# One more mirrored pair of score blocks turned by the DMA, and the second diagonal pair computed whole

## The chip, the cores and the metric

The kernel runs on one core of a Trainium2 chip. The metric is the time of one execution on the device in microseconds (us), the median of three runs.

## The reference

Two layers follow one another. The first is an attention without softmax over 8 batches of 2496 tokens. The second sends each of the 19968 tokens to one of eight experts.

```python
scores = (1.0 / S) * np.matmul(z, z.transpose(0, 2, 1))     # z: 8 x 2496 x 64
attn = np.maximum(scores, 0.0) ** 2
x = (u * np.matmul(attn, v)).reshape(B * S, D)              # u, v: 8 x 2496 x 256
...
expert_idx = np.argmax(x @ w_gate, axis=1)                  # 8 experts
h = np.maximum(xe @ w1[e], 0.0)                             # 256 -> 1024
out[mask] = gate_w[mask, None] * (h @ w2[e])                # 1024 -> 256
```

Two facts of it matter here. The score matrix of a batch is symmetric, since both factors are z: the block of keys A against queries B is the transpose of the block of keys B against queries A. And all inputs are 32-bit floats.

## The kernel before, in words

**Tiles.** A batch has five chunks of queries (`c` = 0 to 4), four of 512 and a last one of 448. Keys come in ten pairs of 128-key blocks (`kp` = 0 to 9), so chunk `cc` of the keys is made of the pairs `2*cc` and `2*cc+1`. One step is one (batch, chunk, pair): `scores` (lines 255 to 336) makes a tile of 2 x 128 keys by `n` queries, `weighted` (lines 338 to 349) multiplies it into the accumulator with v. There are 8 x 5 x 10 = 400 steps. To keep 32-bit accuracy each operand is held as a rounded part and a remainder (`hi` and `lo`), so a step of `weighted` takes 12 matmuls (10 in the step of the last pair).

**A step that computes its scores** has four matmuls into PSUM (lines 309 and 310), two ScalarE activations (Relu on line 318, Square on line 319) into a 32-bit tile `a`, and on VectorE a rounding copy to `hi` (line 320) and a subtraction to `lo` (line 322, or lines 326 and 327 for the last pair).

**A step that takes its scores from the mirror** happens where the keys' chunk `cc` lies before the queries' chunk `c`: the block was computed earlier in the same batch, was kept in one of six slots of SBUF (`s0` to `s5`) and has only to be turned. There are two ways, chosen by `by_dma` (line 251):

- by TensorE: eight 128 x 128 transposes against an identity into PSUM (line 281), then one ScalarE copy to `hi` (line 282) and one VectorE subtraction (line 283). The pairs of chunks (0,3), (0,4), (1,4), (2,4) and (3,4) go this way.
- by the DMA: when the block is computed, ScalarE and VectorE write its upper and lower 16 bits into a tile `th` (lines 333 and 334), and SyncE issues one transposing DMA of that tile into the slot (line 335). When the block is used, ScalarE puts the upper halves back (line 266) and VectorE the lower ones (line 267), then come the copy to `hi` (line 268) and the subtraction (line 269). The pairs (0,1), (0,2), (1,2), (1,3) and (2,3) go this way.

**The diagonal.** Where `cc == c`, the two pairs of a chunk mirror each other in part. With `late` (chunks 1 to 3 of every batch, and chunk 0 of every batch but the first: 31 chunks) the first pair is kept in a tile of its own, `sd`; the second pair computes only its last 256 columns, and the first 256 come from `sd` by four transposes on TensorE (line 315), with a copy and a subtraction of their own (lines 316 and 317).

**Buffers and order.** `ring_f` (name `tf`) has three buffers, `ring_hi` and `ring_lo` four each, the PSUM tiles of the scores (`ps_s`) two, `th` three. `scores` runs three steps ahead of `weighted`. `order_of` (line 228) sets the order of the pairs: the chunk's second diagonal pair goes last, and after the first batch the last chunk goes 0, 2, 3, 4, 5, 6, 7, 8, 9, 1. A scheduler then settles where each instruction stands in its engine's queue, and each queue is worked off in order. SyncE's queue also holds the turning of the output rows (line 393), the loads of z, u and v (lines 120, 150, 137) and the stores of the rows (line 474). The attention is followed by the experts (lines 765 to 819), which use other lines of the kernel.

## Time and profile before

| quantity | value |
|---|---|
| runs | 2329.19, 2334.91, 2337.47 us; median 2334.91 |
| the profiled execution | 2345.85 us, its span 2344.1 us |
| mean granted TensorE clock | 0.992 |
| end of the last chunk's attention in the span | about 1392 us |
| TensorE, VectorE, ScalarE, GpSimd busy | 98%, 70%, 58%, 27% of the span |
| transposing DMAs into slots (line 335) | 80 |
| transposes on TensorE, line 281 and line 315 | 640 and 124 |

The profile is of one execution. PE is TensorE, DVE VectorE, ACT ScalarE, POOL GpSimd, SP SyncE. A matmul's duration in the trace contains a part that overlaps the next matmul, so what a matmul costs is read from one start to the next. `<-` in brackets names what ended the idle time before an instruction. The name of a tile is given without its buffer's number in the trace.

### The profile page before, as it was taken

What the parts mean: (1) busy time and instruction counts of PE and PEld (TensorE: products, weight loads), DVE (VectorE), ACT (ScalarE), POOL (GpSimd) and SP (SyncE); (2) the same over time, 40 slices, a digit from 0 to 9 for tenths busy, and PEclk for the clock granted to TensorE, in tenths of its full rate; (3) what the DMA queues carried; (4) which work ended last, traced back from release to release, by engine and by line L of the source; (5) the groups of instructions that cost most, each with busy time, mean ns of one, the idle gap of its engine ahead of it and who ended that gap; (6) DMA issues with size and microseconds to landing.
All of it is one profiled execution on the core that took longest, in us unless ns stands there. A gap on an engine that the chain in (4) does not pass through costs nothing. (4 is left out here: it accounts for less than half of the span.)

```text
span 2344.1 us, 33779 instructions
## 1 busy us (share of the span) xinstructions
PE 2299.6 (98%) x12448; PEld 1944.4 (83%) x12448; DVE 1652.4 (70%) x2955; ACT 1368.4 (58%) x1864; POOL 625.1 (27%) x637
## 2 busy tenths in 40 slices
PE   9999999999999999999999999899999999999998
PEld 6887888888888888888888887688888888888887
DVE  8877868868868868868878767555565656657554
ACT  7647647647647647657657645354555555546443
POOL 4010110110110211201101234543454435345322
PEclk9999999999999999999999999999999999999999
DMA  6435636536536438447346485655566557456620
GB/s 160 91 64 114 116 59 131 104 67 139 98 72 135 96 68 139 88 72 149 74 73 125 107 156 102 171 145 135 159 163 165 165 128 205 129 145 190 156 77 28
DMA packets 421085, 278.92 MB, mean 119 GB/s; under 512 B 355820, under 2 KB 377850, under 8 KB 411696
## 3 DMA queue, kind: packets, MB, share of 16 engines
q1 hardware_dynamic: 389520, 157.59, 35.5%
q0 software_dynamic: 31392, 119.10, 17.2%
q8 instruction: 99, 1.62, 0.3%
q14 instruction: 74, 0.61, 0.1%
HBM read 149.79 MB, written 43.43 MB: 82 GB/s over the span
## 5 line engine op out<-in xcount | busy, mean ns | idle before, releaser
L349 PE MATMUL acc<-thi,t 128*128 128x512 f32 (+1 forms) x1600 | 617.4, 387 | 0.0
L346 PE MATMUL acc<-thi,t 128*128 128x512 f32 (+1 forms) x1600 | 607.3, 393 | 1.3 <-DVE thi L320 1.3
L348 PE MATMUL acc<-tlo,t 128*128 128x512 f32 (+1 forms) x1520 | 588.8, 387 | 5.2 <-DVE tlo L322 5.2
L784 DVE SCALAR_TENSOR_TENSOR t<-ph,t 128x512 fp32r<-128x512 f32 (+1 forms) x328 | 220.3, 674 | 254.3 <-ACT t L783 218.4
L779 PE MATMUL ph<-thi,t 128*128 128x512 f32 (+2 forms) x1248 | 381.5, 362 | 14.6 <-DVE t L784 12.1
L800 PE MATMUL y<-t,t 128*128 128x512 f32 x1062 | 384.0, 398 | 1.8 <-ACT t L783 1.4
L783 ACT ACTIVATE t<-ph 128x512 fp32r<-128x512 f32 (+1 forms) x328 | 191.7, 588 | 302.6 <-PE ph L779 207.7
L349 PEld LDWEIGHTS acc<-thi,t 128*128 128x128 f32 x1600 | 301.4, 188 | 55.1
L346 PEld LDWEIGHTS acc<-thi,t 128*128 128x128 f32 x1600 | 300.8, 189 | 52.9 <-DVE thi L320 1.7
L348 PEld LDWEIGHTS acc<-tlo,t 128*128 128x128 f32 x1520 | 286.8, 189 | 58.4 <-DVE tlo L322 9.0
L479 POOL DMA_INDIRECT lst<-toks,posi x160 | 180.0, 1125 | 464.5 <-DVE posi L471 423.7
L802 PE MATMUL y<-t,t 128*128 128x256 f32 x1062 | 296.1, 282 | 0.5 <-DVE t L784 0.5
L779 PEld LDWEIGHTS ph<-thi,t 128*128 128x128 f32 x1248 | 226.7, 190 | 58.0 <-DVE t L784 14.0
L800 PEld LDWEIGHTS y<-t,t 128*128 128x128 f32 x1062 | 200.6, 189 | 45.9 <-ACT t L783 1.9
L779 PE MATMUL ph<-tlo,t 128*128 128x512 f32 (+2 forms) x624 | 225.4, 361 | 3.9 <-issue 3.9
L814 POOL DMA_INDIRECT out_dram<-tf,lfidx x136 | 143.3, 1054 | 266.4 <-DVE tf L812 236.5
L802 PEld LDWEIGHTS y<-t,t 128*128 128x128 f32 x1062 | 201.4, 190 | 11.8 <-DVE t L784 1.8
L310 PE MATMUL ps_s<-t,t 128*128 128x512 f32 (+1 forms) x480 | 178.4, 375 | 0.0
L318 ACT ACTIVATE tf<-ps_s 128x1024 f32<-128x1024 f32 (+2 forms) x129 | 117.3, 909 | 76.4 <-PE ps_s L310 39.1
L383 POOL MEMSET rows<- 128x64 int32 x40 | 10.5, 266 | 527.8 <-DMA xrows<-rows 326.6
L714 POOL DMA_INDIRECT rows<-xrows,lfidx x136 | 137.5, 1011 | 44.6 <-issue 37.5
L320 DVE CAST thi<-tf 128x1024 fp32r<-128x1024 f32 (+2 forms) x129 | 81.8, 636 | 87.5 <-ACT tf L319 74.5
(252 smaller groups left out, 4093.0 us busy)
## 6 DMA issues: line engine op xcount, KB each, us to landing
vr<-in_v_dram SPq DMA_DIRECT2D x80, 256.0 KB
xrows<-rows SPq DMA_DIRECT2D x32, 544.0 KB
u<-in_ut_dram SPq DMA_DIRECT2D x32, 512.0 KB
zr<-in_zt_dram SPq DMA_DIRECT2D x38, 256.0 KB
u<-in_ut_dram SPq DMA_DIRECT2D x8, 448.0 KB
xrows<-rows SPq DMA_DIRECT2D x8, 408.0 KB
rows<-th SPq DMA_TRANSPOSE x160
lst<-toks,posi POOLq DMA_INDIRECT x160
```

What stands on the lines that cost most here:

```text
L310: nc.tensor.matmul(ps[:, i, m:n], lhsT=hl_k, rhs=lh_q[:, m:n], start=False, stop=True)
L346: nc.tensor.matmul(acc[d][:, :n], lhsT=vh, rhs=hi[:, i, :n], start=first and i == 0, stop=False)
L348: nc.tensor.matmul(acc[d][:, :n], lhsT=vh, rhs=lo[:, i, :n], start=False, stop=False)
L349: nc.tensor.matmul(acc[d][:, :n], lhsT=vl, rhs=hi[:, i, :n], start=False, stop=last and i == 1)
L479: i = nc.gpsimd.indirect_dma_start(out=lst1, out_offset=bass.IndirectOffsetOnAxis(ap=posi[:m, j:j + 1], axis=0), in_=toks[:m, col + j:col ...
L714: nc.gpsimd.indirect_dma_start(out=xg[:, s, :], out_offset=None, in_=src, in_offset=bass.IndirectOffsetOnAxis(ap=lists[which]["idx"][:, s, ...
L779: nc.tensor.matmul(o, lhsT=w1[:, part, dd, fs], rhs=xx[:, dd, :n], start=p == 0, stop=p == 5)
L783: nc.scalar.activation(hh[:, :m], ph[:, :m], AF.Relu)
L784: nc.vector.scalar_tensor_tensor(hl[:, :m], ph[:, :m], 0.0, hh[:, :m].bitcast(F32), op0=ALU.max, op1=ALU.subtract)
L800: nc.tensor.matmul(y, lhsT=hh[:, cs], rhs=w2[:, f % 2].rearrange("p i d -> p (i d)"), start=f == 0, stop=False)
L802: nc.tensor.matmul(y[:, 0:D], lhsT=hl[:, cs], rhs=w2[:, f % 2, 0, :], start=False, stop=f == NF - 1)
L814: d = nc.gpsimd.indirect_dma_start(out=out, out_offset=bass.IndirectOffsetOnAxis(ap=lists[which]["idx"][:, s, t:t + 1], axis=0), in_=yo[:, ...
```

## The change

`by_dma` now also holds for (3,4): the block that chunk 3 computes for the keys of chunk 4 (pairs 8 and 9) is split into halves and turned by two DMAs while chunk 3 runs, and chunk 4 puts it together again in its steps of the pairs 6 and 7. In the last chunk both copies of line 267's kind are ScalarE's. And the second diagonal pair computes all its columns; `late`, `sd`'s use in the attention, the four transposes and the two instructions of lines 316 and 317 are gone, and the first diagonal pair writes to `ring_f`.

```diff
     def by_dma(c, cc):
-        return c < cc < NC_ - 1 and (c, cc) != (0, 3)
+        return c < cc < NC_ - 1 and (c, cc) != (0, 3) or (c, cc) == (NC_ - 2, NC_ - 1)
...
-            nc.vector.tensor_copy(dst[:, 0], st[:, 1, js])
+            (nc.scalar.copy if c == NC_ - 1 else nc.vector.tensor_copy)(dst[:, 0], st[:, 1, js])
...
-        late = 0 < c < NC_ - 1 or b and c == 0
...
-        elif late and kp % 2 == 0:
-            sd = ring_sd().bitcast(F32).rearrange("p s r -> p (s r)")[:, 0:2 * QC]
-            a = stored[b, c, c] = sd.rearrange("p (i n) -> p i n", i=2)
         else:
             a = ring_f()
...
-        m = HQ if cc == c and late and kp % 2 else 0
         for i in range(2):
...
-            nc.tensor.matmul(ps[:, i, m:n], lhsT=hl_k, rhs=hl_q[:, m:n], start=True, stop=False)
-            nc.tensor.matmul(ps[:, i, m:n], lhsT=hl_k, rhs=lh_q[:, m:n], start=False, stop=True)
-        if m:
-            st = stored.pop((b, c, c))
...
-                    nc.tensor.transpose(ps[:, i, r * P:(r + 1) * P], st[:, r, HQ + i * P:HQ + (i + 1) * P], ident)
-            nc.scalar.copy(hi[:, :, 0:m], ps[:, :, 0:m])
-            nc.vector.tensor_tensor(lo[:, :, 0:m], ps[:, :, 0:m], hi[:, :, 0:m].bitcast(F32), op=ALU.subtract)
+            nc.tensor.matmul(ps[:, i, :n], lhsT=hl_k, rhs=hl_q[:, :n], start=True, stop=False)
+            nc.tensor.matmul(ps[:, i, :n], lhsT=hl_k, rhs=lh_q[:, :n], start=False, stop=True)
```

The activations, the rounding copy and the subtraction behind these lines lose their `m` likewise and work on all `n` columns.

The change moves instructions in three queues. The new kernel has twelve lines less, so line 318 of before is line 306 there, 319 is 307, 333 is 321, 335 is 323, 346 is 334, 393 is 381, 431 is 419 and 474 is 462; lines 266 to 268 and 282 keep their numbers.

On TensorE, the second diagonal pair of chunk 1 of the first batch before; `t` are the parts of z and of v, 128x256 is the half that is computed:

```order
L349 MATMUL acc_520<-thi,t_362 128x512
L309 MATMUL ps_s<-t_143 128x256
L310 MATMUL ps_s<-t_144,t_143 128x256
L309 MATMUL ps_s<-t_143 128x256
L310 MATMUL ps_s<-t_144,t_143 128x256
L315 MATMUL ps_s<-ident,sd 128x128 x4
L346 MATMUL acc_519<-thi,t_476 128x512
```

And now:

```order
L337 MATMUL acc_520<-thi,t_362 128x512
L304 MATMUL ps_s<-t_143 128x512
L305 MATMUL ps_s<-t_144,t_143 128x512
L304 MATMUL ps_s<-t_143 128x512
L305 MATMUL ps_s<-t_144,t_143 128x512
L334 MATMUL acc_519<-thi,t_476 128x512
```

The four matmuls have twice the columns, and the four transposes behind them are gone.

On ScalarE, the end of chunk 3 and the start of chunk 4 in the second batch before; the first four rows are the pairs 8 and 9 of chunk 3, whose block goes straight into slot `s1`, the next three the second diagonal pair, and `2x448` are the casts of mirrored steps of chunk 4:

```order
L318 ACTIVATE s1_3049<-ps_s_3048 128x1024
L319 ACTIVATE s1_3049<-s1_3049 128x1024
L318 ACTIVATE s1_3049<-ps_s_3078 128x1024
L319 ACTIVATE s1_3049<-s1_3049 128x1024
L316 CAST thi_3100<-ps_s_3102 128x2x256
L318 ACTIVATE tf_3103<-ps_s_3102 128x2x256
L319 ACTIVATE tf_3103<-tf_3103 128x2x256
L282 CAST thi_3139<-ps_s_3141 128x2x448
L431 ACTIVATE ex_2923<-dl_3132 128x32
L282 CAST thi_3165<-ps_s_3167 128x2x448
```

And now, from pair 9 on:

```order
L306 ACTIVATE tf_3046<-ps_s_3045 128x1024
L307 ACTIVATE tf_3046<-tf_3046 128x1024
L321 COPY th_3056<-tf_3046 128x2x512
L306 ACTIVATE tf_3075<-ps_s_3074 128x1024
L307 ACTIVATE tf_3075<-tf_3075 128x1024
L282 CAST thi_3105<-ps_s_3107 128x2x448
L266 COPY tf_3276<-s1_3011 128x1024
L267 COPY tf_3276<-s1_3011 128x1024
L266 COPY tf_3329<-s1_3011 128x1024
L267 COPY tf_3329<-s1_3011 128x1024
L419 ACTIVATE ex_2885<-dl_3098 128x32
L282 CAST thi_3131<-ps_s_3133 128x2x448
```

The four copies out of slot `s1`, which belong to the sixth and seventh step of chunk 4, stand right behind the cast of its first step and ahead of that of its second. So it is in the batches 0 to 6; in the last batch they stand ahead of the first cast too.

On SyncE, the stretch of chunk 3 in the second batch before, from the last transposing DMA of the pair (2,3):

```order
L335 DMA_TRANSPOSE s3_2640<-th_2738 128x16x128
L120 DMA zr_3338<-in_zt_dram 128x512
L474 DMA xrows_72<-rows_2586 128x4x272
L150 DMA u_2965<-in_ut_dram 128x2x512
L393 DMA_TRANSPOSE rows_2921<-th_3039 128x4x128 x4
L120 DMA zr_3667<-in_zt_dram 128x512
L474 DMA xrows_72<-rows_2921 128x4x272
L150 DMA u_3306<-in_ut_dram 128x2x448
```

And now:

```order
L323 DMA_TRANSPOSE s3_2608<-th_2706 128x16x128
L120 DMA zr_3298<-in_zt_dram 128x512
L462 DMA xrows_72<-rows_2554 128x4x272
L150 DMA u_2927<-in_ut_dram 128x2x512
L381 DMA_TRANSPOSE rows_2883<-th_3001 128x4x128 x4
L323 DMA_TRANSPOSE s1_3011<-th_3021 128x16x128
L120 DMA zr_3621<-in_zt_dram 128x512
L323 DMA_TRANSPOSE s1_3011<-th_3056 128x16x128
L462 DMA xrows_72<-rows_2883 128x4x272
L150 DMA u_3272<-in_ut_dram 128x2x448
```

One new transposing DMA stands between the turned rows and the load of z, the other behind that load.

More of the change, by code (lines that the diff above doesn't have):

```diff
@@ L308, in scores @@
             hl_k = ztiles[b, k // 4][0][:, (k % 4) * P:(k % 4 + 1) * P]
-            nc.tensor.matmul(ps[:, i, m:n], lhsT=hl_k, rhs=hl_q[:, m:n], start=True, stop=False)
-            nc.tensor.matmul(ps[:, i, m:n], lhsT=hl_k, rhs=lh_q[:, m:n], start=False, stop=True)
-        if m:
-            st = stored.pop((b, c, c))
-            for i in range(2):
-                for r in range(2):
-                    nc.tensor.transpose(ps[:, i, r * P:(r + 1) * P], st[:, r, HQ + i * P:HQ + (i + 1) * P], ident)
-            nc.scalar.copy(hi[:, :, 0:m], ps[:, :, 0:m])
-            nc.vector.tensor_tensor(lo[:, :, 0:m], ps[:, :, 0:m], hi[:, :, 0:m].bitcast(F32), op=ALU.subtract)
-        nc.scalar.activation(a[:, :, m:n], ps[:, :, m:n], AF.Relu)
-        nc.scalar.activation(a[:, :, m:n], a[:, :, m:n], AF.Square)
-        nc.vector.tensor_copy(hi[:, :, m:n], a[:, :, m:n])
+            nc.tensor.matmul(ps[:, i, :n], lhsT=hl_k, rhs=hl_q[:, :n], start=True, stop=False)
+            nc.tensor.matmul(ps[:, i, :n], lhsT=hl_k, rhs=lh_q[:, :n], start=False, stop=True)
+        nc.scalar.activation(a[:, :, :n], ps[:, :, :n], AF.Relu)
+        nc.scalar.activation(a[:, :, :n], a[:, :, :n], AF.Square)
+        nc.vector.tensor_copy(hi[:, :, :n], a[:, :, :n])
         if kp < NKP - 1:
-            nc.vector.tensor_tensor(lo[:, :, m:n], a[:, :, m:n], hi[:, :, m:n].bitcast(F32), op=ALU.subtract)
+            nc.vector.tensor_tensor(lo[:, :, :n], a[:, :, :n], hi[:, :, :n].bitcast(F32), op=ALU.subtract)
         else:
```

## The prediction

> **What bounds the kernel now.** I read the busy times first, then the stretches, then TensorE's own waits, and last the timeline at the steps that the change touches. The page's first part names the engine with the least room:
>
> ```profile
> PE 2299.6 (98%) x12448; PEld 1944.4 (83%) x12448; DVE 1652.4 (70%) x2955; ACT 1368.4 (58%) x1864; POOL 625.1 (27%) x637
> ```
>
> An average hides stages, so here are stretches (length, then the busy time of PE, PEld, DVE, ACT, POOL, then the granted clock and the DMA): the attention, the experts' stage, ten microseconds at the start of the second batch, and about its chunks 3 and 4.
>
> ```profile
> 0.00:1392.00 1392.00, 1379.15 (x7529) 1154.36 (x7530) 1094.12 (x1890) 873.33 (x993) 228.07 (x251) 1.00 0.53 103
> 1392.00:2344.00 952.00, 920.45 (x4921) 790.04 (x4919) 558.32 (x1065) 495.03 (x872) 397.04 (x386) 0.99 0.53 143
> 200.00:210.00 10.00, 8.21 (x50) 6.53 (x51) 7.78 (x15) 1.75 (x2) 1.69 (x3) 0.83 0.85 184
> 280.00:315.00 35.00, 35.00 (x192) 29.03 (x191) 27.05 (x45) 20.83 (x22) 4.17 (x5) 1.00 0.48 71
> 315.00:350.00 35.00, 35.00 (x221) 31.18 (x221) 21.00 (x38) 11.85 (x17) 4.03 (x5) 1.00 0.48 55
> ```
>
> In the attention TensorE is idle for 12.9 of 1392 us, in the experts' stage for 31.6 of 952. In chunks 3 and 4 it has no idle time at all, while ScalarE has 14 and 23 us of 35 to spare and VectorE 8 and 14. What TensorE does wait for inside the attention is short (total, times, longest):
>
> ```profile
> PE acc L348 <- DVE tlo L322: 5.2, 4, 2.3
> PE ps_s L309 <- ACT sd L318: 1.5, 2, 0.8
> ```
>
> So a microsecond of work taken from TensorE in the attention is a microsecond of time, unless the work that replaces it makes TensorE wait.
>
> **The turned pair: what TensorE saves.** The transposes before the change, and one such step of chunk 4 in the timeline (start, duration):
>
> ```profile
> L281 PE MATMUL ps_s<-ident,s 128*128 128x128 f32 x640 | 86.9, 275 | 0.2 <-DVE tlo L283 0.2
> L315 PE MATMUL ps_s<-ident,sd 128*128 128x128 f32 x124 | 18.6, 272 | 0.0
> ```
>
> ```profile
> 331.09 1.03 PE L281 MATMUL ps_s<-ident,s 128*128 128x128 f32 x8
> 331.88 0.45 PE L346 MATMUL acc<-thi,t 128*128 128x448 f32 x1
> 332.37 0.37 PE L349 MATMUL acc<-thi,t 128*128 128x448 f32 x1
> 333.59 0.37 PE L349 MATMUL acc<-thi,t 128*128 128x448 f32 x1
> ```
>
> From 332.37 to 333.59 lie six matmuls, 0.203 us each; that is the pace, not the 0.37 of the duration column. From 331.09 to 332.37, 1.28 us, lie eight transposes and two matmuls, so the eight cost 1.28 - 0.41 = 0.87 us, the slower start of the matmul behind them included. Five pairs of chunks share the 640 transposes; (3,4) has 128 of them, 16 times eight. The saving is 16 x 0.87 = 14.0 us, all on the path.
>
> **The diagonal: what TensorE pays and saves.** The second diagonal pair in chunk 1 of the first batch:
>
> ```profile
> 71.69 0.39 PE L348 MATMUL acc<-tlo,t 128*128 128x512 f32 x1
> 73.96 0.39 PE L349 MATMUL acc<-thi,t 128*128 128x512 f32 x1
> 74.18 0.28 PE L309 MATMUL ps_s<-t 128*128 128x256 f32 x1
> 74.66 0.60 PE L315 MATMUL ps_s<-ident,sd 128*128 128x128 f32 x4
> 75.01 0.48 PE L346 MATMUL acc<-thi,t 128*128 128x512 f32 x1
> 75.33 0.39 PE L348 MATMUL acc<-tlo,t 128*128 128x512 f32 x1
> ```
>
> Ten matmuls of 512 columns take 73.96 - 71.69 = 2.27 us, 0.227 each. The half pair takes 74.66 - 74.18 = 0.48 us for four matmuls and 75.33 - 74.66 - 0.227 = 0.44 us for four transposes, 0.92 together. Whole, it takes 4 x 0.227 = 0.91 us. The 124 transposes are four each in 31 places: 31 x 0.015 = 0.5 us saved. For TensorE this edit is a draw.
>
> **What ScalarE and VectorE get.** The groups of like instructions (busy in total, mean ns of one):
>
> ```profile
> L266 ACT COPY tf<-s 128x1024 uint16<-128x1024 uint16 x80 | 105.3, 1367 | 14.8 <-DVE tlo L269 11.5 <-ACT thi L282 2.2 <-DVE tlo L322 0.7
> L268 ACT CAST thi<-tf 128x1024 fp32r<-128x1024 f32 x80 | 82.9, 1057 | 49.6 <-PE acc L349 42.1 <-DVE tlo L269 6.3 <-issue 1.3
> L282 ACT CAST thi<-ps_s 128x896 fp32r<-128x896 f32 x64 | 58.0, 907 | 117.9 <-PE ps_s L281 55.7 <-PE acc L349 53.0 <-remote 9.3
> L333 ACT COPY th<-tf 128x1024 uint16<-128x1024 uint16 x80 | 84.1, 1052 | 0.7
> L334 DVE COPY th<-tf 128x1024 uint16<-128x1024 uint16 x80 | 56.4, 705 | 0.6 <-ACT tf L319 0.6
> L283 DVE TENSOR_TENSOR tlo<-ps_s,thi 128x896 fp32r<-128x896 f32 x64 | 69.8, 1090 | 62.9 <-ACT thi L282 59.2 <-issue 2.8
> ```
>
> A used step of (3,4) in chunk 4 gives ScalarE two copies of 1.37 us (the second stands on VectorE elsewhere; it has the same shape, so I take the same price) and a cast between 0.91 and 1.06 in place of one of 0.91: 2.7 to 2.9 us more. Making the step in chunk 3 adds 1.05 us to ScalarE and 0.71 to VectorE. VectorE's subtraction of 1.09 stays. Per batch that is 5.4 to 5.8 us for ScalarE in chunk 4, which has 23 free, and 2.1 and 1.4 us for ScalarE and VectorE in chunk 3, which have 14 and 8 free. The diagonal:
>
> ```profile
> L316 ACT CAST thi<-ps_s 128x512 fp32r<-128x512 f32 x31 | 18.2, 586 | 67.8 <-PE ps_s L315 40.1 <-PE acc L348 19.5 <-DVE tlo L322 6.7
> L318 ACT ACTIVATE tf<-ps_s 128x512 f32<-128x512 f32 x31 | 18.5, 598 | 29.6 <-DVE tlo L317 29.5
> L319 ACT ACTIVATE tf<-tf 128x512 f32<-128x512 f32 x31 | 19.8, 640 | 0.3
> L318 ACT ACTIVATE sd<-ps_s 128x1024 f32<-128x1024 f32 x31 | 31.9, 1028 | 9.6 <-PE ps_s L310 9.6
> L319 ACT ACTIVATE sd<-sd 128x1024 f32<-128x1024 f32 x31 | 33.0, 1064 | 0.6
> ```
>
> ScalarE's three instructions of 0.59, 0.60 and 0.64 become two of 1.03 and 1.06, 0.27 us more; the wait of line 318 for line 317 (29.5 us in all, off the path) goes, so PSUM comes free sooner. No engine becomes the bound on average. All of this costs nothing as long as the step is ready when TensorE gets to it.
>
> **Is it ready?** This decides the sign. ScalarE's queue now has four copies out of the slot between the first and the second cast of chunk 4; the first of them waits until both DMAs have landed, and the casts of the steps that TensorE needs next are queued behind it. In the second batch before:
>
> ```profile
> 310.80 5.15 SPq L393 DMA_TRANSPOSE rows<-th  x4
> 317.06 0.47 SPq L120 DMA_DIRECT2D zr<-in_zt_dram  x1
> ```
>
> ```profile
> 314.33 1.03 ACT L318 ACTIVATE s<-ps_s 128x1024 f32<-128x1024 f32 x1 [1.51 <-PE ps_s L310]
> ```
>
> The row at 314.33 is the Relu of pair 9. With its Square and the copy to `th` (1.03 + 1.06 + 1.05) ScalarE's half is there at 317.5, VectorE's about 0.7 to 1 later. SyncE is done with the rows at 315.95, issues the DMA of pair 8, then z, then that of pair 9: at 318.5, or 320 if the first holds the queue longer. For landing, the tightest place of the trace is the pair (2,3) in the last batch, where the second DMA is issued and its user starts:
>
> ```profile
> 1321.15 1.86 SPq L335 DMA_TRANSPOSE s<-th  x1
> ```
>
> ```profile
> 1326.52 1.37 ACT L266 COPY tf<-s 128x1024 uint16<-128x1024 uint16 x1 [0.36 <-DVE tlo L322]
> ```
>
> It did not wait for the DMA, so landing takes at most 5.4 us from issue. The copies then start by 323.9 to 325.4. The deadline: the cast and subtraction of chunk 4's second step (0.91 + 1.09) follow four copies (5.5), and they must free PSUM for the transposes that stood at 331.09. These now stand seven matmuls into chunk 4, so about 331.1 + 7 x 0.203 = 332.5. The copies must start by 325.0. That leaves between 1.1 us to spare and 0.4 us too late; a delay of 0.4 in eight batches is 3 us. I take 0.5 us, nearer to the early end, since the 5.4 is an upper bound. In the last batch all four copies stand ahead of the first cast, one more chance of a wait.
>
> **The sum.** 14.0 + 0.5 - 0.5 = 14.0 us. The profiled execution took 2345.85 us, so its like would take 2331.9; the median of the runs is 2334.91, 10.9 lower, and the forecast from it is 2320.9, which I round to 2321. The experts' stage, which TensorE fills too, starts where the attention ends and moves along.
>
> **The rivals.** About 0.3%, 7 us, is what a measurement of this kernel can tell from no change.
>
> *Landing is late: slower.* The rows of the DMA's issue and of the costliest wait of TensorE:
>
> ```profile
> L335 SPq DMA_TRANSPOSE s<-th x80: 1317/1997/7074, 21.7 to 1321.2; - x80
> ```
>
> ```profile
> 201.79 0.50 PE L348 MATMUL acc<-tlo,t 128*128 128x512 f32 x1 [1.80 <-DVE tlo L322]
> ```
>
> The longest hold of the queue is 7.07 us against 1.86 in the tight place, so a landing of 5.4 + 5.2 = 10.6 us can be, with 318.5 as issue 4.1 us behind the deadline. A wait of TensorE is followed by a lower clock: in the stretch of 201.79 it was 0.83 over 10 us, 1.7 us more. That is 8 x (4.1 + 1.7) = 46 us lost, 32 net: 2367. It turns the sign from 14.5 / 8 = 1.8 us of loss per batch on: a landing 8.3 us after an issue at 318.5. Against it: the median hold is 2.0, and the DMA's share around chunk 3 is 0.48. Chance 0.11. The Trainium skill (VectorE: DVE Perf Modes, The three transpose paths) speaks for this rival: it gives 390 ns on TensorE and 1309 ns by the DMA for a 128x128 transpose and advises TensorE where PSUM will do; one of these DMAs turns 16 such blocks, which by estimate from that page would land after 21 us, 14.5 us behind the deadline, and make the kernel some 100 us slower. The trace does not agree: its sixteen blocks landed within 5.4 us. By the Trainium skill (TensorE: Matmul & The Clock Gate, HAM oscillation) only idle gaps over about 3.4 us lower the clock; here one of 1.80 did, or fell into the wrong part of its window.
>
> *Part is given back: no change.* The diagonal's first tile now comes out of the three buffers of `tf`, and so does the new turned pair. ScalarE already waits for VectorE to let one go (the row of line 266: 11.5 us in 8 times, 1.4 each). If one such wait per batch reaches TensorE whole, 8 x 1.4 = 11.5 us go, and 2332 remains. For it speaks that VectorE is the engine that TensorE waits for now (5.2 us); against it, that scores run three steps ahead. Chance 0.15.
>
> *The new order also mends the wait at 201.79.* Then 1.8 + 1.7 us more are saved: 2317. Chance 0.10.
>
> **How the numbers follow.** The forecast has 0.64. Range: below, the mended wait less the 4 us by which runs of one kernel differ: 2313. Above, the part given back plus 4: 2336. That leaves out the late landing and little else. Faster by over 0.3% (under 2327.9) are the forecast and the mended wait, 0.74; the same 0.15; slower 0.11.
>
> **What would show it.** Right: 512 transposes of line 281 and none of line 315; 96 DMAs into slots; TensorE's idle time in the attention near 13 us; the attention ending near 1378. The four copies of chunk 4 start about 324 in the second batch's terms, and TensorE's first transposes after them wait for nothing. Wrong: waits of ScalarE on the slot's DMA of more than 2 us a batch, followed by TensorE waiting for line 282 or 283 at the start of chunk 4, or a granted clock below 1.0 there; or TensorE waiting on `tf` in chunks 1 and 2.

## The result, and the profile after

The changed kernel is slower: a median of 2363.22 us (2358.62 to 2365.51) against 2332.05 us (2328.51 to 2337.47) of the kernel before, ratio 1.0129 (95% interval 1.0100 to 1.0158). Measured once more on another chip it was 1.0079 (1.0056 to 1.0102). The forecast was 2321.0 us, 2313 to 2336.

The work went as the change says, 252 transposes fewer (12448 to 12196 instructions of TensorE; the matmuls of the diagonal are wider, not more):

```profile
PE 2289.5 (97%) x12196; PEld 1925.0 (81%) x12196; DVE 1665.7 (70%) x2940; ACT 1448.3 (61%) x1881; POOL 649.1 (27%) x637
```

The stretches show where the time is. First the kernel before, then the changed one, each from the start of the span to the first matmul of the experts (length, then TensorE's busy time):

```profile
0.00:1404.60 1404.60, 1391.75 (x7594) 1166.06 (x7595) 1104.65 (x1913) 881.53 (x1005) 228.07 (x251) 1.00 0.54 104
```

```profile
0.00:1426.20 1426.20, 1382.99 (x7342) 1147.78 (x7343) 1114.79 (x1890) 960.63 (x1022) 250.16 (x251) 0.99 0.57 107
```

TensorE is busy 8.8 us less and idle 43.2 instead of 12.85 us, 30.4 more. That is the 21.6 us by which the attention is longer; what follows takes 2.3 us less (937.2 and 939.5 us). In the changed kernel's chain that ended last, TensorE has 74% of the span, and the loads of v (`vr`) have 4%:

```profile
PE ph L767 15%; PE acc L337 12%; PE acc L334 12%; PE acc L336 11%; PE y L788 10%; PE y L790 5%; DMA vr<-in_v_dram 4%; PE ps_s L304 3%; PE ps_s L305 3%; PE ps_s L281 2%; DVE thi L308 1%; SPq L733 1%; DVE tlo L310 1%; DMA th<-rows 1%; DVE t L144 1%
```

TensorE's waits up to the experts (total, times, longest) name three places. Lines 336, 310, 334, 304 and 306 are 348, 322, 346, 309 and 318 of before:

```profile
PE ps_s L281 <- ACT tf L306: 13.0, 6, 3.8
PE acc L336 <- DVE tlo L310: 12.6, 10, 2.3
PE acc L334 <- ACT thi L282: 9.4, 2, 9.1
```

The first is in chunk 4: transposes of a later pair wait for the Relu of a diagonal pair to let go of its PSUM tile. The second, 5.2 us before, is in the next batch's chunk 0, mostly 12 to 13 us behind its first matmul. The third is at the start of the last batch's chunk 4. They make 13.0 + (12.6 - 5.2) + 9.4 = 29.8 of the 30.4 us.

**Chunk 4 of the second batch** shows the first one from its cause on. ScalarE after:

```profile
319.72 0.91 ACT L282 CAST thi<-ps_s 128x896 fp32r<-128x896 f32 x1 [1.47 <-PE ps_s L281]
321.86 1.36 ACT L266 COPY tf<-s 128x1024 uint16<-128x1024 uint16 x1 [1.23 <-DVE cd L429]
...
325.51 1.35 ACT L267 COPY tf<-s 128x1024 uint16<-128x1024 uint16 x1
326.73 0.22 ACT L419 ACTIVATE ex<-dl 128x32 f32<-128x32 f32 x1
326.85 1.69 ACT L282 CAST thi<-ps_s 128x896 fp32r<-128x896 f32 x2
```

The copies wait for no DMA here and start 3.1 us ahead of the deadline that the prediction worked out. But the second cast starts 7.1 us after the first; before, it was 3.6:

```profile
321.59 0.91 ACT L282 CAST thi<-ps_s 128x896 fp32r<-128x896 f32 x1 [0.39 <-PE ps_s L281]
...
325.21 0.91 ACT L282 CAST thi<-ps_s 128x896 fp32r<-128x896 f32 x1 [1.22 <-PE ps_s L281]
```

VectorE has the subtraction of that step next, and the last operations of chunk 2's routing behind it, up to `posi` (line 459), which GpSimd's scatters into `lst` wait for. VectorE and GpSimd after:

```profile
327.77 1.09 DVE L283 TENSOR_TENSOR tlo<-ps_s,thi 128x896 fp32r<-128x896 f32 x1 [5.47 <-ACT thi L282]
...
330.49 0.16 DVE L459 CAST posi<-posr 128x4 int32<-128x4 f32 x1
```

```profile
330.92 0.96 POOL L467 DMA_INDIRECT lst<-toks,posi  x1 [26.00 <-DVE posi L459]
```

The same places before:

```profile
326.15 1.09 DVE L283 TENSOR_TENSOR tlo<-ps_s,thi 128x896 fp32r<-128x896 f32 x1 [1.75 <-ACT thi L282]
```

```profile
329.45 0.96 POOL L479 DMA_INDIRECT lst<-toks,posi  x1 [22.69 <-DVE posi L471]
```

Chunk 4's first matmul is at 331.88 before and 329.22 after, so the scatters come 2.4 us ahead of it before and 1.7 us behind it now. SyncE loads the next batch's v meanwhile, and ScalarE rounds each piece (line 142). The third piece, after, then before:

```profile
349.43 0.62 ACT L142 CAST t<-vr 128x512 fp32r<-128x512 f32 x1 [8.66 <-DMA vr<-in_v_dram]
349.96 1.04 ACT L376 COPY th<-x 128x1024 uint16<-128x1024 uint16 x1
350.90 0.91 ACT L306 ACTIVATE tf<-ps_s 128x896 f32<-128x896 f32 x1
```

```profile
348.93 0.62 ACT L142 CAST t<-vr 128x512 fp32r<-128x512 f32 x1 [5.23 <-DMA vr<-in_v_dram]
349.45 1.04 ACT L388 COPY th<-x 128x1024 uint16<-128x1024 uint16 x1
350.40 0.91 ACT L318 ACTIVATE tf<-ps_s 128x896 f32<-128x896 f32 x1
```

The third piece is there 20.2 us into chunk 4 instead of 17.05, and the Relu of pair 8 stands behind its cast in both kernels. Before, TensorE still had transposes to do and came to the scores of the pairs 8 and 9 at 347.46 and 349.28, so it did not need that Relu's tile yet. Now it comes to them at 341.40 and 344.64. The scores of pair 8, before, then after:

```profile
347.46 0.36 PE L309 MATMUL ps_s<-t 128*128 128x448 f32 x1
```

```profile
341.40 0.36 PE L304 MATMUL ps_s<-t 128*128 128x448 f32 x1
```

So the next transposes need the tile that the Relu still holds:

```profile
347.68 0.37 PE L337 MATMUL acc<-thi,t 128*128 128x448 f32 x1
351.87 1.97 PE L281 MATMUL ps_s<-ident,s 128*128 128x128 f32 x8 [3.82 <-ACT tf L306]
353.49 0.72 PE L334 MATMUL acc<-thi,t 128*128 128x448 f32 x1
354.01 0.57 PE L336 MATMUL acc<-tlo,t 128*128 128x448 f32 x1
354.38 0.57 PE L337 MATMUL acc<-thi,t 128*128 128x448 f32 x1
```

Behind the wait the matmuls come every 0.37 us and not every 0.203, until 356.99. From 351.87 to 357.32 TensorE does eight transposes and ten matmuls, which at the prediction's prices (0.87 and 0.203) take 2.90 us and not 5.45: by this estimate the wait costs some 2.5 us more than it is long. ScalarE's waits for v between 190 and 1390 us, before and after:

```profile
ACT t L142 <- DMA vr<-in_v_dram: 50.0, 18, 5.3
```

```profile
ACT t L142 <- DMA vr<-in_v_dram: 76.6, 24, 8.7
```

**In the last batch** the copies stand ahead of chunk 4's first cast as well, and there the turned block is late: SyncE's issue of its two transposing DMAs lasts from 1370.07 to 1386.23, ScalarE waits for them, and TensorE for ScalarE:

```profile
1370.07 16.16 SPq L323 DMA_TRANSPOSE s<-th  x2
```

```profile
1388.43 1.33 ACT L266 COPY tf<-s 128x1024 uint16<-128x1024 uint16 x1 [13.22 <-DMA s<-th]
```

```profile
1394.12 0.74 PE L334 MATMUL acc<-thi,t 128*128 128x448 f32 x1 [9.08 <-ACT thi L282]
```

### The profile page after: what moved, and what is told of

Its sections match the earlier page's. It is cut to its first block, busy times and chain, and to the rows that moved or that the text cites. A ratio compares the mean times of both kernels' runs of the same rounds, so it can differ in the third digit from the quotient of the medians.

```text
span 2363.4 us, 33432 instructions
## 1 busy us (share of the span) xinstructions
PE 2289.5 (97%) x12196; PEld 1925.0 (81%) x12196; DVE 1665.7 (70%) x2940; ACT 1448.3 (61%) x1881; POOL 649.1 (27%) x637
## 3 DMA queue, kind: packets, MB, share of 16 engines
q0 software_dynamic: 31392, 119.10, 17.9%
## 4 chain that ended last, share of the span: by engine, by line
PE 74%; DMA 7%; issue 6%; DVE 6%; ACT 3%; SPq 2%; POOL 1%; another core or an unknown queue 1%; POOLq 0%; DVEq 0%; ACTq 0%
PE ph L767 15%; PE acc L337 12%; PE acc L334 12%; PE acc L336 11%; PE y L788 10%; PE y L790 5%; DMA vr<-in_v_dram 4%; PE ps_s L304 3%; PE ps_s L305 3%; PE ps_s L281 2%; DVE thi L308 1%; SPq L733 1%; DVE tlo L310 1%; DMA th<-rows 1%; DVE t L144 1%
## 5 line engine op out<-in xcount | busy, mean ns | idle before, releaser
L336 PE MATMUL acc<-tlo,t 128*128 128x512 f32 (+1 forms) x1520 | 588.6, 387 | 12.6 <-DVE tlo L310 12.6
L467 POOL DMA_INDIRECT lst<-toks,posi x160 | 200.8, 1255 | 446.7 <-DVE posi L459 404.7
L306 ACT ACTIVATE tf<-ps_s 128x1024 f32<-128x1024 f32 (+1 forms) x176 | 178.6, 1015 | 87.2 <-PE ps_s L305 80.3
L310 DVE TENSOR_TENSOR tlo<-tf,thi 128x1024 fp32r<-128x1024 f32 (+1 forms) x160 | 194.5, 1216 | 3.0
L307 ACT ACTIVATE tf<-tf 128x1024 f32<-128x1024 f32 (+1 forms) x176 | 185.1, 1052 | 4.2
L305 PE MATMUL ps_s<-t,t 128*128 128x512 f32 (+1 forms) x480 | 186.6, 389 | 0.0
L308 DVE CAST thi<-tf 128x1024 fp32r<-128x1024 f32 (+1 forms) x176 | 123.7, 703 | 69.4 <-ACT tf L307 56.9
```

The costliest lines, as they stand in the source:

```text
L305: nc.tensor.matmul(ps[:, i, :n], lhsT=hl_k, rhs=lh_q[:, :n], start=False, stop=True)
L307: nc.scalar.activation(a[:, :, :n], a[:, :, :n], AF.Square)
L310: nc.vector.tensor_tensor(lo[:, :, :n], a[:, :, :n], hi[:, :, :n].bitcast(F32), op=ALU.subtract)
L336: nc.tensor.matmul(acc[d][:, :n], lhsT=vh, rhs=lo[:, i, :n], start=False, stop=False)
L467: i = nc.gpsimd.indirect_dma_start(out=lst1, out_offset=bass.IndirectOffsetOnAxis(ap=posi[:m, j:j + 1], axis=0), in_=toks[:m, col + j:col ...
```

## The experiments

The theory from the two profiles, A: TensorE waits because ScalarE stands still for v's load with work behind it that TensorE needs. The rivals: ScalarE has too much to do in chunk 4 with four copies more; the additional transposing DMAs slow v down; the diagonal's edit makes the loss. The letters in the expectations are explained in each. The first four expectations give times of the chip of the first measurement, where the kernel before took 2332.05 us; on theirs it took 2341.72, so their times are read here as ratios. All ratios are to the kernel before on the same chip, which took 2341.72 us beside the first four kernels, then 2322.19, 2337.24, 2321.83 and 2331.70 us. Each edit is shown against the changed kernel, and `...` marks lines that are left out.

### The two edits apart

```diff
-        return c < cc < NC_ - 1 and (c, cc) != (0, 3) or (c, cc) == (NC_ - 2, NC_ - 1)
+        return c < cc < NC_ - 1 and (c, cc) != (0, 3)
...
```

> Only the diagonal computed whole, the pair (3,4) by TensorE as before. Theory A (the queue of ScalarE in chunk 4: the cast of the next batch's v waits there for its DMA and holds the Relu behind it): as before, 2332 within 7 us, because none of this is touched. Theory B (the turned pair lands late): as before too. Theory C (the diagonal's tile out of the three buffers of tf holds the steps up): 2350 or more.

Measured: 2334.13 us, 0.9961 (0.9947 to 0.9976), a little faster than all three theories have it. The other half keeps the line above and takes back the diagonal's lines (`late`, `m`, the four transposes):

> Only the pair (3,4) by the DMA, the diagonal in halves as before. Theories A and B: all of the loss, 2357 to 2369, with a stall of TensorE of some 9 us in the last batch and 4 to 7 us lost per chunk 4 elsewhere. Theory C: 2332 less 14, 2318, or at most 2335.

Measured: 2358.81 us, 1.0068 (1.0044 to 1.0091), less than the 1.011 to 1.016 of A and B. Alone, the turned pair is a loss and the whole diagonal a gain. But the two do not add up: with both, the kernel is at 1.0079 and 1.0129, not faster than with the turned pair alone, and why the diagonal's gain does not show there is open. And the stall of 9 us in the last batch, which A and B expected here too, is not there; the section on the last batch comes back to it. With the diagonal alone TensorE is idle 9.4 us up to the experts:

```profile
0.00:1394.20 1394.20, 1384.82 (x7470) 1158.85 (x7471) 1112.36 (x1882) 902.53 (x974) 231.17 (x251) 1.00 0.53 105
```

### v's loads

A third buffer for v, in a tile that only the warm-up uses:

```diff
+        fetched[0] += 1
+        if b and fetched[0] % 3 == 0:
+            vraw[b, kp] = sb.tile([P, 2, D], F32, name="vr3", tag="lp")
+        else:
-        vraw[b, kp] = sb.tile([P, 2, D], F32, name="vr", bufs=2)
+            vraw[b, kp] = sb.tile([P, 2, D], F32, name="vr", bufs=2)
```

> The changed kernel with a third buffer for the raw v (it takes the warm-up's tile, so nothing else is moved), so that the third load of v in chunk 4 need not wait for the first cast and is issued before the stores and scatters. Theory A: the longest wait of ScalarE on v (6 to 9 us per batch) goes, the stalls of TensorE on the transposes for PSUM (13.0 us in 6 places, and the lower clock behind them) go, 15 to 30 us are won: 2333 to 2348. Theory B: no change, 2358 to 2368, since nothing of the turned pair is touched.

Measured: 2356.12 us, 1.0062 (1.0035 to 1.0089), at the slow end of A's range (1.000 to 1.007). The waits for the Relu are gone, as A has it, and chunk 4, from its first matmul of 448 columns to the first of 512 behind it, takes 32.6 us in the mean of seven batches (36.7 with the change as it is); but chunks 0 to 3 take some 3 us more in most batches. In part that is only counted elsewhere: the scheduler had put the scores of the next chunk 0 in other places on TensorE, and one pair's four matmuls, 0.9 us, stand in chunk 0 and no longer in chunk 4. Next, the rounding copy of v moved to GpSimd, in the changed kernel and, as a control, in the kernel before:

```diff
-        nc.scalar.copy(vt[:, 0], vr)
+        (nc.gpsimd.tensor_copy if b else nc.scalar.copy)(vt[:, 0], vr)
```

> The changed kernel with the rounding copy of v (line 142) on GpSimd from the second batch on. Theory A (ScalarE stands still in its wait for v's load, 76.6 us in 24 waits, with the Relu of chunk 4's diagonal behind it, and TensorE's transposes, which used to cover that, are gone): TensorE's waits for the Relu in chunk 4 (13.0 us in six) go and with them the low clock behind them; chunk 4 takes 32 to 33 us in place of 35 to 39; the wait for the copies in the last batch (9 us) stays, since it does not hang on v. Ratio to the kernel before 0.996 to 1.004. Theory B (ScalarE simply has too much to do in chunk 4 with four copies of 1.37 us, wherever the wait is): only the 0.6 us of each cast is given back, chunk 4 stays at 34 us or more, ratio 1.006 to 1.012.

> The kernel before with v's copy on GpSimd, and nothing else: a control. Theory A: ScalarE's wait for v (50.0 us in 18 waits there) is covered by TensorE's transposes, so taking it away brings nothing: ratio 0.997 to 1.003. Theory B: the wait costs there as well, and the gain is like that of the same edit in the changed kernel, 0.6% or more: ratio under 0.995. A shift of the scheduler's order alone can move either by about 0.3%.

Measured: 2339.06 us, 1.0065 (1.0048 to 1.0083), and for the control 2332.92 us, 1.0052 (1.0033 to 1.0071). Taking ScalarE's 50 us of waiting for v out of the kernel before brings no gain, as A says, but the control cannot show that they cost nothing, since the move itself costs 0.5%, which neither theory has. In its profile TensorE waits for VectorE at more places, most of them 24 to 37 us behind the first matmul of a chunk 0:

```profile
PE acc L346 <- DVE thi L320: 6.7, 11, 1.3
```

They do not explain the 0.5%: all idle time up to the experts is 14.1 us, 1.2 more than before. So a move that should cost nothing can shift the time by 0.5%, and between ratios as close as that only the waits in the profiles can tell theories apart. In the changed kernel the waits for the Relu go with v's copy, but the ratio stays outside A's range and inside B's: v is not all of it.

### The last batch

```diff
-        return c < cc < NC_ - 1 and (c, cc) != (0, 3) or (c, cc) == (NC_ - 2, NC_ - 1)
+        return c < cc < NC_ - 1 and (c, cc) != (0, 3) or (c, cc) == (NC_ - 2, NC_ - 1) and b < B - 1
...
```

> The changed kernel, but the last batch turns (3,4) on TensorE as before. There ScalarE has the four copies ahead of the first cast of chunk 4, waits 13.2 us for the DMA, and TensorE 9.1. Theories A and B: this stall goes, less the 1.75 us of transposes that come back: 7 to 9 us won, 2354 to 2357. If the stall is only moved into the experts' stage, nothing is won: 2360 to 2366.

Measured: 2353.23 us, 1.0036 (1.0017 to 1.0055), better than the 1.009 to 1.011 of A and B. With the last batch's pair turned by TensorE its wait of 9 us is gone; chunk 4 of the other batches stays slow (34.9 us in the mean).

The wait needs a late block as well as the copies ahead of the cast. (The next section has the late block without the copies there, and no wait.) With the turned pair alone the copies stand there too, but SyncE is done with the two DMAs in 4.4 us, ScalarE waits 3.96 us for them, and no wait of TensorE there is over 0.65 us:

```profile
1366.23 4.40 SPq L335 DMA_TRANSPOSE s<-th  x2
```

What differs is where GpSimd's gathers of rows for the experts stand. In the changed kernel they run ahead of the two DMAs' issue and beside it, with the turned pair alone only behind it:

```profile
1367.74 1.05 POOL L702 DMA_INDIRECT rows<-xrows,laidx  x1 [0.30 <-issue]
```

```profile
1369.40 1.25 POOL L714 DMA_INDIRECT sd<-xrows,laidx  x1 [12.40 <-ACT thi L316]
```

All kernels here that turn this pair by the DMA in the last batch go the same way. With gathers ahead, SyncE's issue of the two lasts 8.4 to 16.2 us (eleven profiles of ten kernels); with none ahead, 4.4 to 5.8 us (four kernels). No run moves the gathers alone, so that they are the cause is not shown.

### The place of the copies

The four copies of chunk 4 held where the program has them, so that the scheduler does not move them ahead:

```diff
+            def halves():
+                nc.scalar.copy(dst[:, 1], st[:, 0, js])
+                (nc.scalar.copy if c == NC_ - 1 else nc.vector.tensor_copy)(dst[:, 0], st[:, 1, js])
+            pinned(halves) if c == NC_ - 1 else halves()
```

> The changed kernel with the four copies of chunk 4 held at their place in the program, behind the casts of the steps ahead of them; nothing is taken from ScalarE. In its queue the exponential now stands behind the first cast of chunk 4, two copies stand behind each of the first and second casts of v, and the Relu of pair 8 ahead of the third cast of v. Theory A: the routing starts some 3 us earlier in the batch, the scatters and with them v's load are earlier, and what still waits for v has no Relu of pair 8 behind it: chunk 4 takes 32 to 34 us, and in the last batch the wait of 13 us for the turned block goes. Ratio to before 0.992 to 1.000. Theory B (too much work on ScalarE in chunk 4): the copies now stand among the casts and delay them more; chunk 4 at 35 us or more, ratio 1.006 to 1.015. Theory C (the two more transposing DMAs slow v's load down by themselves): v's waits stay at 70 us and more, ratio above 1.004.

Measured: 2315.77 us, 0.9973 (0.9949 to 0.9997), in A's range. The same DMAs, the same copies on the same engine, and 1% or more comes back. No wait for a Relu is left among TensorE's waits, and chunk 4 takes 30.8 us in five of seven batches. Of the 5.9 us that this is below 36.7, some 1.8 (0.91 and 0.87 at the prediction's prices) are four score matmuls and eight transposes that stand in chunks 0 to 3 here. In the last batch TensorE waits for no cast, although SyncE's issue of the two DMAs lasts 14.1 us. The longest wait of TensorE that is left, in total, and ScalarE's wait for v, which is less than before the change:

```profile
PE acc L338 <- DVE tlo L312: 15.1, 12, 2.3
```

```profile
ACT t L142 <- DMA vr<-in_v_dram: 35.3, 20, 3.6
```

So neither ScalarE's load nor the DMAs by themselves make the loss, but the place of the copies. What is held up by it? First the exponential, put ahead of the copies with `tc.issue_after`, all else word for word the same; and half of the copies given back to VectorE:

```diff
+            with ExitStack() as behind:
+                if c == NC_ - 1:
+                    behind.enter_context(tc.issue_after(exp_at[-1]))
...
```

> The changed kernel with one thing moved: the exponential of the routing stands ahead of the four copies of chunk 4 in ScalarE's queue and not behind them; the copies still stand ahead of the second cast, and the rest of the queue is word for word the same. Theory A1 (the copies hold up the routing; its scatters come later and with them v's load; ScalarE's third cast then waits for v with the Relu of pair 8 behind it): v's load lands some 3 us earlier in the batch, as before the change, TensorE's waits for the Relu in chunk 4 (13.0 us in six) fall under 4 us, chunk 4 takes 33 to 34 us in place of 35 to 39; ratio to before 1.001 to 1.007. Theory A2 (the copies hold up the casts behind them, and these, not the routing, make the rest of ScalarE's work late): nothing changes, chunk 4 at 35 to 39 us, ratio 1.010 to 1.015.

```diff
-            (nc.scalar.copy if c == NC_ - 1 else nc.vector.tensor_copy)(dst[:, 0], st[:, 1, js])
+            nc.vector.tensor_copy(dst[:, 0], st[:, 1, js])
```

> The changed kernel with the lower halves of chunk 4's turned pair copied by VectorE, as in the other chunks: two copies instead of four stand ahead of the exponential and the second cast in ScalarE's queue, 2.7 us instead of 5.5. Theory A (what stands in ScalarE's queue ahead of its routing and casts is the loss): about half of chunk 4's loss goes, 33 to 35 us; ratio to before 1.003 to 1.009. Theory B (VectorE, which TensorE waits for in chunk 0, has no room either): two copies of 0.75 us a batch more on VectorE; chunk 4 stays at 35 us or more, ratio 1.012 to 1.018.

Beside them the change once more, as it is:

> The changed kernel itself once more, beside the two above on the same chip, so that each of them is compared with it and not through the kernel before: all theories expect the ratio of the first measurement, 1.010 to 1.016, with chunk 4 at 35 to 39 us and a wait of about 9 us of TensorE in the last batch.

Measured: 2357.45 us, 1.0081 (1.0055 to 1.0107) with the exponential first; 2362.14 us, 1.0105 (1.0082 to 1.0128) with two copies on VectorE; 2355.64 us, 1.0079 (1.0056 to 1.0102) for the change, somewhat less than expected and than at first. In this second profile of the change chunk 4 takes 35.0 us in the mean, the waits for the Relu are 6.1 us and the wait in the last batch is 7.3. A1 falls, though the ratio lies between the two ranges: with the exponential ahead of the copies nothing else is earlier. VectorE waits as long as without the edit (5.36 and 5.47 us), and the scatters still start 2.1 us behind chunk 4's first matmul (330.11 and 327.99):

```profile
326.42 1.09 DVE L286 TENSOR_TENSOR tlo<-ps_s,thi 128x896 fp32r<-128x896 f32 x1 [5.36 <-ACT thi L285]
```

```profile
330.11 0.97 POOL L470 DMA_INDIRECT lst<-toks,posi  x1 [26.42 <-DVE posi L462]
```

VectorE waits for the cast, and the routing's operations stand behind it. Giving two copies to VectorE missed A's range too, and lies below B's: in its profile the waits for the Relu are 9.4 us, between those of the change's two profiles, and TensorE waits 6.0 us at one place of the last batch.

### The two queues

The routing of chunk 2 two steps earlier, so that on VectorE its operations stand ahead of that subtraction:

```diff
-        bg.extend([nothing] * (4 if b == B - 1 and c == NC_ - 1 else 2) + route(b * S + q0, n, ns, logits_of, xr))
+        bg.extend([nothing] * (4 if b == B - 1 and c == NC_ - 1 else 0 if c == NC_ - 3 else 2) + route(b * S + q0, n, ns, logits_of, xr))
```

> The changed kernel with the routing of chunk 2 two steps earlier, so that on VectorE its last operations stand ahead of the subtraction of chunk 4's second mirrored step and no longer behind it; ScalarE's queue at the four copies is the same but for the exponential. Theory S (the copies delay the second cast; VectorE waits for it with the routing behind, 6 us; the scatters then run into v's load): the scatters leave 5 us or more earlier, 2 us ahead of chunk 4's start or before in place of 2.4 after it; ScalarE's waits for v fall from about 70 us to 50 or under; TensorE's waits for the Relu of pair 8 (6 to 13 us) fall under 3. Ratio to the kernel before 0.999 to 1.006. Theory Q (v's load is late whatever the scatters do): waits for v 65 us or more, ratio 1.007 to 1.013.

Measured: 2324.08 us, 1.0006 (0.9985 to 1.0028), theory S's range and apart from the change's 1.0079. The ten times spread from 2312.63 to 2335.79 us, and the profile is of the fastest. In it the score matmuls at the end of chunk 4 and in the next chunk 0 stand where the changed kernel has them. The scatters of the second batch start 3.1 us ahead of chunk 4 (325.55), ScalarE waits for v as little as before the change, and TensorE for the Relu once:

```profile
322.46 0.97 POOL L467 DMA_INDIRECT lst<-toks,posi  x1 [0.57 <-issue]
```

```profile
ACT t L142 <- DMA vr<-in_v_dram: 50.5, 24, 5.6
```

```profile
PE ps_s L281 <- ACT tf L306: 0.8, 1, 0.8
```

The copies are still where the change put them. Chunk 4 takes 33.1 us in the mean, where the change's two profiles have 36.7 and 35.0. But not all of the gain is this chain's: the edit also moved GpSimd's gathers in the last batch behind the two transposing DMAs, SyncE's issue of them lasts 5.8 us, and the wait of 7 to 9 us there is gone too. Now the other end: the third cast of v one step later, behind the Relu.

```diff
...
+            if j == 4:
+                pinned(lambda: split_v(b + 1, order_of(b + 1, 0)[2]))
             fetch_v(b + 1, order_of(b + 1, 0)[j])
-            if j:
+            if j and j != 3:
```

> The changed kernel with one copy moved: ScalarE's third cast of v stands one step later, behind the Relu and Square of the diagonal's pair 8 and no longer ahead of them. Nothing is done to the copies, the routing or the loads. If the order in ScalarE's queue carries the wait to TensorE: v's load is as late as before the edit, ScalarE's waits for v stay within 15 us of 70, and TensorE's waits for the Relu in chunk 4 (6 to 13 us) are gone; ratio 1.000 to 1.007. If something else makes the Relu late: the waits stay, ratio 1.007 to 1.013. The fourth load of v comes a step later with it, which can cost up to 1 us a batch.

> The changed kernel with the two moves together: the routing two steps earlier, and the third cast of v behind the Relu. The four copies stay where the change has them, ahead of the second cast. If these two queues carry all of chunk 4's loss: chunk 4 without waits for the Relu, ratio 0.995 to 1.002, close to the copies held at their place (0.9973). If the copies cost by themselves, through the second and third cast: TensorE still loses 1 us or more in chunk 4 and the last batch keeps its wait of some 9 us for the turned block: ratio 1.003 to 1.010.

Measured: 2336.70 us, 1.0064 (1.0042 to 1.0085), and with both moves 2343.64 us, 1.0088 (1.0056 to 1.0119). The waits for the Relu in chunk 4 go in both, so the cast ahead of it did carry the wait. ScalarE's waits for v fell to 45.0 us with the cast alone, where 55 to 85 were expected; the cast comes later itself. But it is paid elsewhere: in the next chunk 0 TensorE now waits for VectorE, 1.7 us in most batches with both moves. And in the profile with both, TensorE waits 17.9 us once near the hand-over to the experts, where ScalarE has a copy out of another transposing DMA ahead of a Square:

```profile
1402.71 1.33 ACT L746 COPY x<-th 128x1024 uint16<-128x1024 uint16 x1 [23.08 <-DMA th<-sd]
1403.91 0.93 ACT L307 ACTIVATE tf<-tf 128x896 f32<-128x896 f32 x1
```

The expectation of 0.995 to 1.002 for both failed, with these two in its profile. So the chain is what made TensorE wait in chunk 4, but that these two queues carry all of the loss is not shown.

### Both in the best form

> The changed kernel with both edits: the four copies held at their place, and v's copy on GpSimd. Theory A: neither loss is left, and the 14 us that the prediction gave to the turned pair show beside the 9 us of the whole diagonal: chunk 4 at 31 to 32.5 us, chunks 0 to 3 at 139 to 140 us, ratio to before 0.988 to 0.994, the fastest of all. Theory B: between 1.000 and 1.010. If VectorE's waits at the start of the next batch's chunk 0 (line 336 on line 310, about 1.4 us a batch) are a loss of their own, 0.994 to 0.998.

Measured, with the copies held and v's copy on GpSimd: 2308.93 us, 0.9947 (0.9929 to 0.9965), the fastest, and faster than both kernels. It misses A's range and lies in the one that takes VectorE's waits in chunk 0 as a loss of their own. Its stretch up to the experts:

```profile
0.00:1385.20 1385.20, 1372.29 (x7332) 1143.04 (x7333) 1126.31 (x1888) 924.50 (x951) 274.52 (x321) 1.00 0.59 111
```

Beside the whole diagonal alone TensorE is busy 1384.82 - 1372.29 = 12.5 us less. But it is idle 12.9 us and not 9.4. What is left are waits for VectorE, mostly 24 to 26 us into chunk 0; two kernels tried to take them away, and a third to get the scatters out of the way of v. The score matmuls of chunk 0 held at their place in the program:

```diff
+        pinned(multiply) if b and c == 0 else multiply()
```

> The kernel with both edits (copies held at their place, v's copy on GpSimd) and the score matmuls of chunk 0, from the second batch on, held at their place too: behind 6, 14 and 24 matmuls of the accumulators, not behind 6, 14 and 62. If TensorE's waits for VectorE at the start of chunk 0 (11.4 us in 15, with a lower clock behind each) come from the order of the scores, they fall under 6 us and the ratio to before is 0.988 to 0.993. If VectorE has too much to do there in any order (v's remainders, the rows, the routing), the waits stay and the ratio is 0.993 to 0.998.

VectorE's subtraction for v on GpSimd as well:

```diff
-        eng = nc.gpsimd if b == 0 and kp > 1 else nc.vector
+        eng = nc.gpsimd if b or kp > 1 else nc.vector
```

> The changed kernel with the copies held at their place and all of v's splitting (copy and subtraction) on GpSimd from the second batch on, so that VectorE is relieved of 10 subtractions of 0.69 us a batch. If VectorE's crowding is what is left at the start of chunk 0 (TensorE's waits for line 312, 15.1 us in twelve with the copies held): those waits fall under 6 us, ratio 0.987 to 0.993. If GpSimd, where such a subtraction takes 1.8 us, becomes late with v's parts or with the scatters queued behind them: new waits of TensorE for v's parts or a later routing, ratio 0.995 to 1.005.

And the earlier routing added to the fastest, with the whole diagonal alone beside it:

> The fastest kernel so far (copies held at their place, v's copy on GpSimd: 0.9947) with the routing of chunk 2 two steps earlier. With the copies held, no cast is late and the routing waits for nothing there; what can be gained is only that the scatters leave before v's loads. If those loads still lose time to the scatters (GpSimd waits 8 us for the third load): ratio 0.990 to 0.994. If not: the same as without the move, 0.993 to 0.997. If VectorE's routing operations in the place of a step's operations make TensorE wait: above 0.997.

> The whole diagonal alone once more, beside the kernel above on the same chip, to tell what the turned pair is worth beyond it. The first measurement gave 0.9961 (0.9947 to 0.9976), so 0.994 to 0.998. If the turned pair, with its copies in order, brings its 14 us, the kernel above is 0.4% or more faster than this one; if the waits at the start of chunk 0 eat it, the two are within 0.2%.

Measured: 2353.93 us, 1.0075 (1.0050 to 1.0099); 2325.35 us, 1.0019 (0.9999 to 1.0038); 2330.22 us, 1.0003 (0.9986 to 1.0019); and the diagonal alone 2327.48 us, 0.9979 (0.9971 to 0.9988). None of the three helps. Held scores make it worse, with TensorE's waits for lines 314 and 312 at 23.1 us, and with all of v on GpSimd the like waits are 17.5 us and not under 6. The last pair leaves a question open. The fastest kernel's near twin is slower than the diagonal alone beside it, although its attention is 4.1 us shorter in the profile (first matmul of the experts at 1389.5 and 1393.6). Its twelve times spread from 2323.06 to 2342.28 us, the diagonal's eleven from 2324.10 to 2328.98. Whether the turned pair is worth more than the diagonal alone in every execution is not settled.

## Why the prediction was wrong, point by point

**The turned pair saves 14.0 us of TensorE: right as work, a little too much.** In the best form TensorE is busy 12.5 us less than with the diagonal alone; in the mean chunk 4 takes 31.0 us there and 32.8 without the turned pair, where 14.0 / 8 is 1.75. But "all on the path" did not hold: chunks 0 to 3 of the same two kernels take 140.9 and 139.4 us from the second batch on, so most of what a chunk 4 gains is lost again in the next chunks. In the changed kernel TensorE is busy 1382.99 us for the same instructions that take the fastest kernel 1372.29. The 10.7 us between them go with a lower granted clock (0.99 and 1.00 over these stretches), as in the 0.37 us a matmul behind the wait above.

**The diagonal is a draw: nearer to right than the times look.** That edit alone gave 0.9961 and 0.9979, and in its first profile TensorE is busy 6.9 us less and idle 3.5 us less. Up to 5.1 of the 6.9 are no work. Before's profile has a lower granted clock at two places (0.83 over 200 to 210 us, 1.7 us; 0.72 over 1378 to 1390 us, 3.4 us), and the other has 1.00 at both. What is left is an estimate of 1.8 us, where 0.5 was forecast. The rival that mends the wait at 201.79 came true in one of that kernel's two profiles; in the other TensorE waits 1.66 us there.

**No engine becomes the bound on average: right**, and it did not help. Held at their place, the same copies leave TensorE no wait for ScalarE up to the experts.

**"Is it ready?" was answered for the wrong step.** The deadline was worked out for the turned pair's own data and for the second cast and its subtraction, as far as TensorE's next transposes need them. In the second batch it held: copies at 321.86, deadline 325.0, and the transposes, at 330.63, wait for nothing. The step that failed is the sentence ahead of it, "All of this costs nothing as long as the step is ready when TensorE gets to it". The step was ready, and it cost. Its four copies, placed early, stood ahead of a cast that they had nothing to do with. The prediction followed that cast only to TensorE, and not to what else stood in VectorE's queue behind its subtraction. VectorE waited for the cast with the routing behind it; the routing's scatters then left 1.7 us behind chunk 4's start and not 2.4 ahead of it; v's third piece came later; ScalarE waited for v with a Relu behind it; and the transposes that had kept TensorE busy during that wait were what the change removed.

How far the runs show it: copies moved, 0.9973 and no wait for a Relu; exponential alone, nothing; routing moved, 1.0006, scatters earlier, waits for v 50.5 us and not 76.6 or 69.0; v's cast moved, the wait for the Relu gone and other waits in its place. One link is argued: that the scatters themselves slow the load. The runs show that the two move together, and none delays the scatters alone. That an engine works its queue off in order is what the Trainium skill (TensorE: Matmul & The Clock Gate, Architectural detail: the array is 16× 32×32, not 1× 128×128) says of ScalarE and VectorE, strict FIFO. The trace agrees: VectorE stood idle 5.47 us with the routing's operations queued behind the one that waited.

**The rival *Landing is late*** had the sign, and its mechanism in one place. "In the last batch all four copies stand ahead of the first cast, one more chance of a wait" has no term of its own in the sum; it cost 9.1 us and 7.3 us in the two profiles of the change, where the block was late too. In the other batches ScalarE waited for the block as well, but TensorE next to nothing for line 282 (9.4 us in all, 9.1 of them here). ScalarE's waits for the block (total, times, longest):

```profile
ACT tf L266 <- DMA s<-th: 22.3, 4, 13.2
```

**The rival *Part is given back*** named VectorE and `tf`; TensorE's added 7.4 us of waits for VectorE are in chunk 0. The order of the scores on TensorE changed there from 6 and 14 matmuls ahead to 7 and 24. The fastest kernel has 6 and 14 again, and there other waits for VectorE, later in chunk 0, make some 7 us. The diagonal alone has 6 and 14 too, and from the second batch on it waits for VectorE 0.2 us in one profile and 1.7 in the other. So the order alone does not explain these waits; what makes VectorE late there stays open.

**The sum.** -14.0 was forecast. In the profiled executions the attention became 21.6 us longer, 8.8 us less of busy time and 30.4 more of waiting. These profiled executions differ by 19.7 us and the medians by 31, mostly since the profiled execution of before lies 13.8 us above its median.

## What to carry to other kernels

An instruction that is ready early can be worse than one that comes late: where a scheduler puts work with its data ready, look at what it now stands ahead of on its engine, and follow that to the next engine's queue until TensorE. Work that is taken from the engine that sets the time was also the cover for somebody's wait, so list the waits beside it before counting the saving. Where the place decides, hold the instruction at its place in the program and measure that beside the edit.

## What the runs showed of the hardware

The slower pace behind a wait does not go by the wait's length alone. In the changed kernel a wait of 2.11 us, at 1054.57, is followed by none (granted clock 1.00 from 1054 to 1060). And two waits of the same kind, 1.54 us at 905.83 and 1.43 us at 731.17, are followed by these stretches (the third-last number is the granted clock):

```profile
905.00:911.00 6.00, 5.17 (x16) 4.08 (x17) 5.88 (x10) 0.98 (x1) 5.18 (x3) 0.72 0.78 200
731.00:737.00 6.00, 5.83 (x26) 4.83 (x27) 5.88 (x10) 0.00 (x0) 5.08 (x4) 1.00 0.78 197
```

The first lost another 1.7 us, the second 0.1. By the Trainium skill (TensorE: Matmul & The Clock Gate, HAM oscillation) the clock goes down after an idle gap of over about 3.4 us. The trace does not agree for the 1.54 us, and does for the 2.11.

A transposing DMA of a turned block landed within 5.4 us of its issue at the tight place that the prediction quotes. In the last batch the pair's two, issued from 1370.07 on, were there at 1388.43, over 18 us after the first was issued. The same two DMAs took SyncE 4.4 to 5.8 us to issue in the four kernels that gather no rows for the experts just ahead of them, and 8.4 to 16.2 us in the ten that do.
